# A second place for the first part's values, interleaved products of its last two units, and sixteen weight conversions moved into stage two

## The chip, the cores and the metric

The kernel runs on one core of a Trainium2 chip. The metric is the device time of one execution in microseconds (us). Of the kernel before, three executions are given, 863.11, 866.15 and 866.83 us, with a median of 866.15 us; one further execution was recorded by the profiler.

## The reference, cut to what matters

Three layers run one after the other: block-causal attention (4 batches, 8 heads, 576 tokens, 64 wide), a dense layer with a leaky ReLU, and a layer that sends each token to one of eight experts. The change concerns the second layer alone:

```
x = attn_out.transpose(0, 2, 1, 3).reshape(2304, 512)
h = x @ w_in                     # w_in 512 x 2048
g = maximum(0.01 * h, h)
y = g @ w_out                    # w_out 2048 x 512
```

The weights `w_in` and `w_out` come as 64-bit floats, and the kernel converts them on the chip.

## The kernel before, in words

**The split of the dense layer.** The 2048 columns of `w_in` (and rows of `w_out`) are cut into 512 columns that are done in stage one, beside and just after the attention (the "first part" of the layer, weights `wi_a`, `wo_a`), and 1536 that are done in stage two (`wi_b`, `wo_b`). Stage two's weights lie in six tiles `wbt0` to `wbt5` and fall again into a first, second and third part of 512 columns: `wbt0`/`wbt1` are its first part's `w_in`/`w_out`, `wbt2`/`wbt4` its second's, `wbt3`/`wbt5` its third's. `wbt0` and `wbt1` are also the attention's places for its queries and keys.

**A conversion** (`split64`, `split_words`, L391 to L420) loads 512 KB into one of three `raw` tiles (L398, SP's queue) and makes a high and a low fp32r tile of it. The steps are two on ScalarE (L413, L414), three on VectorE (L415, L416, L417), one on GpSimd (L418), then the high part on ScalarE (L419) and the low part on VectorE (L420). One part has eight conversions, four of `w_in` and four of `w_out`. While the list `gate` holds instructions, every instruction of a conversion stands behind the one of its engine in that list.

**A unit** of stage one is 384 tokens; there are six, 0 to 5 (`half_a_steps`). `mm1(f)`, four of them, each multiply 12 products into a PSUM bank `ph` (three products for each of four 128-row pieces: high x high, high x low, low x high), and `leaky` (L437 to L439) makes the values `gA` of it: ScalarE scales (L437, into a tile `cv2`), VectorE takes the maximum (L438), ScalarE rounds to the high part (L438 ACT), GpSimd subtracts for the low part (L439). `mm2(t)`, three of them, multiply `gA` with `wo_a`, 12 products each, into a bank `po`, which ScalarE copies out (L489) and SP's queue stores (L490). There is one pair of tiles `gA` for all units, so a unit's `leaky` waits for the unit before to have read it in all its `mm2`. Units 4 and 5 take their `ph` from the four banks with the tag `ps` that the attention uses too, and their small tiles from a pool `tr` with two buffers each.

**The order of the work.** Attention steps, units 0 to 3 and conversions carry due times and are sorted by them (`todo`). A scheduler that simulates a timeline then orders the instructions of each engine, so products of two groups can come interleaved. The attention's last pair ends with `pv` products (L285), the sum of its two halves (L298 on ScalarE, L299 on VectorE), a rounding (L301) and a low part (L302 on GpSimd); these write the last tokens of `xT`, which units 4 and 5 read. In the list the four `w_out` conversions of stage two's first part come at due times 33.0 to 33.6, between the attention's last steps, which end at 34.3. Then the attention's pools are closed, the pool `WB` (`wbt2` to `wbt5`) and the pool `tr` are opened, and units 4 and 5 follow one after the other, with five conversions of the second part between their steps (L535 to L540).

**Stage two** (L1036 to L1076) goes over 72 pairs of a unit of 384 tokens and a 128-column piece (the first 36 go to three units in turns, four pieces at a time): `b_mm1` (12 products and `leaky`) and, two steps later, `b_mm2` (9 products into `acc`). In two of three steps a conversion is taken from the list `wb` (L1043); when it is empty, `load_rows` (L598 to L604) loads the rows of the routing weights that the logits (L662) need from step 31 on. The pieces of the second part are first used in step 12, those of the third in step 24.

Of the kernel before, what the change touches and what calls it, by code (L numbers as in the profile page):

```python
# [11 lines left out]
F32R = mybir.dt.float32r  # L12
# [13 lines left out]
def run_all(steps):  # L26
    for s in steps:
        s()
# [318 lines left out]
def attention_moe_kernel(  # L347
# [21 lines left out]
    NFA, NFB = FA // 128, FB // 128  # L369
# [4 lines left out]
    BT = TB * 128  # L374
# [47 lines left out]
    def moe_weight_steps(f0, n, wi, wo, pin=False):  # L422

        steps = []
        for a in range(0, n, 4):
            for c in range(ND):
                steps.append(lambda a=a, c=c: split64(
                    wi[0][:, c, a * 128 : a * 128 + 512], wi[1][:, c, a * 128 : a * 128 + 512],
                    w_in[c * 128 : (c + 1) * 128, f0 + a * 128 : f0 + a * 128 + 512], pin))
            for f in range(a, a + 4):  # L430
                steps.append(lambda f=f: split64(
                    wo[0][:, f], wo[1][:, f], w_out[f0 + f * 128 : f0 + (f + 1) * 128], pin))
        return steps

    def leaky(pool, ph, N, gh, gl, bufs, name="u", width=0):
        u = pool.tile([128, max(N, width)], F32, name=name, bufs=bufs)[:, 0:N]
        nc.scalar.activation(out=u, in_=ph, func=AF.Copy, scale=0.01)  # L437
        return [nc.vector.tensor_tensor(out=u, in0=ph, in1=u, op=ALU.max), nc.scalar.copy(gh, u),  # L438
                nc.gpsimd.tensor_tensor(out=gl, in0=u, in1=gh.bitcast(F32), op=ALU.subtract)]  # L439

    def three(ps, a, b, first, last):

        n = len(a)
        m = 0
        for (ah, al), (bh, bl) in zip(a, b):
            for x, y in ((ah, bh), (ah, bl), (al, bh)):
                nc.tensor.matmul(ps, x, y, start=first and m == 0, stop=last and m == 3 * n - 1)  # L447
                m += 1
# [3 lines left out]
    right = ExitStack()  # L452
    ps1 = p1.enter_context(tc.tile_pool(name="ps1", bufs=1, space=PSUM))
    M1 = p1.enter_context(tc.tile_pool(name="m1", bufs=1))
    wi_a = [M1.tile([128, ND, FA], F32R, name=f"wia{i}") for i in range(2)]
    wo_a = [M1.tile([128, NFA, D], F32R, name=f"woa{i}") for i in range(2)]
    BAS = ((0, 256), (256, 320))
    gA = [M1.tile([128, NFA, BT], F32R, name=f"gA{i}") for i in range(2)]

    WA = ctx.enter_context(tc.tile_pool(name="wa", bufs=1, side="right"))  # L460
    wbt = [WA.tile([128, 2, 4 * 512], F32R, name=f"wbt{i}") for i in range(2)]
# [7 lines left out]

    where, a_ends = [CV, 512, 3], []  # L470

    def half_a_steps(u, tag="mm", bufs=2):

        o = u % 3 * BT

        def mm1(f):
            ph = ps1.tile([128, 512], F32, name="ph", tag=tag, bufs=bufs)[:, 0:BT]
            fs = slice(f * 128, f * 128 + 128)
            three(ph, [(wi_a[0][:, c, fs], wi_a[1][:, c, fs]) for c in range(ND)],
                  [(xT[0][:, c, o : o + BT], xT[1][:, c, o : o + BT]) for c in range(ND)], True, True)  # L480
            a_ends[:] = leaky(where[0], ph, BT, gA[0][:, f], gA[1][:, f], where[2], "cv2", where[1])

        def mm2(t):
            po = ps1.tile([128, 512], F32, name="po", tag="mm", bufs=2)
            ts = slice(t * 128, t * 128 + 128)
            three(po, [(gA[0][:, f, ts], gA[1][:, f, ts]) for f in range(NFA)],
                  [(wo_a[0][:, f], wo_a[1][:, f]) for f in range(NFA)], True, True)
            st = where[0].tile([128, 512], F32, name="cv3", bufs=where[2])
            a_ends[:] = [nc.scalar.copy(st, po)]  # L489
            nc.sync.dma_start(part_d[u * BT + t * 128 : u * BT + t * 128 + 128], st)  # L490

        return [lambda f=f: mm1(f) for f in range(NFA)] + [lambda t=t: mm2(t) for t in range(TB)]
# [8 lines left out]
    todo = att.steps(dst, LAG)  # L501
# [3 lines left out]
    for u, (t0, t1, n) in enumerate(((10.35, 17.15, 7), (17.15, 19.1, 4), (21.5, 26.2, 7), (26.35, 33.1, 7))):  # L505
        ha = half_a_steps(u)
        todo += [(t0 + (t1 - t0) * j / n, s) for j, s in enumerate(ha[:n])]
        todo += [(t1 + 0.7 * j, s) for j, s in enumerate(ha[n:])]
# [3 lines left out]
    end = per * B  # L512
# [4 lines left out]
    def wb_steps(a):  # L517

        wi, wo = ([wbt[at[a]][:, i].rearrange("p (c w) -> p c w", c=4) for i in range(2)] for at in (wi_at, wo_at))
        return moe_weight_steps(FA + a * 512, 4, wi, wo)  # L520

    wb = wb_steps(0)
    todo += [(end - 0.5 + 0.2 * j, s) for j, s in enumerate(wb[:4])]
    todo += [(end + 1 + 0.2 * j, s) for j, s in enumerate(wb[4:])]
    run_all(s for _, s in sorted(todo, key=lambda x: x[0]))
    right.close()
    gate[:] = a_ends
    right = ExitStack()
    WB = right.enter_context(tc.tile_pool(name="wb", bufs=1, side="right"))
    wbt += [WB.tile([128, 2, 4 * 512], F32R, name=f"wbt{i}") for i in range(2, 6)]  # L530
    behind = ExitStack()
    where[1:] = BT, 2
    where[0] = behind.enter_context(tc.tile_pool(name="tr", bufs=1, side="right"))
    wb = wb_steps(1) + wb_steps(2)
    for j, step in enumerate(half_a_steps(4, "ps", 4) + half_a_steps(5, "ps", 4)):  # L535
        step()
        if j in (4, 6, 8, 10, 12):

            gate[:] = a_ends
            wb.pop(0)()  # L540
    behind.close()
    p1.close()


# [289 lines left out]
    def load_expert(e):  # L834
# [4 lines left out]
        if k_ < 3:  # L839
            x, y = ((wo_at[0], wo_at[1]), (wi_at[2], wo_at[2]), (wi_at[0], wi_at[1]))[k_]  # L840
            a, b = ((WA if t < 2 else WB).tile([128, 2, 4 * 512], F32, name=f"wbt{t}").rearrange("p i w -> p (i w)") for t in (x, y))
            a, b = a.rearrange("p (c w) -> p c w", w=F2), b.rearrange("p (c k w) -> p c k w", k=2, w=D)
# [198 lines left out]
    for i in range(len(seq) + lag):  # L1041
# [11 lines left out]
        f = i - (len(seq) - NFB)  # L1053
# [16 lines left out]
        if i >= lag:  # L1070
            n, f = seq[i - lag]
# [29 lines left out]
    end = finish()  # L1101
# [110 lines left out]
```

## Time and profile before

| what | value |
|---|---|
| three executions | 863.11, 866.15, 866.83 us (median 866.15) |
| the profiled execution | 863.9 us, span 862.1 us from first to last instruction |
| PE busy in the span | 795.8 us (92%), 4100 products |
| mean granted TensorE clock | 0.980 |
| end of the attention's last product to stage two's first | 317.5 to 357.94 us |
| stage two up to its logits | 358 to 480 us, PE busy 121.57 of 122 us |

PE is TensorE's multiplying, PEld its weight load, DVE VectorE, ACT ScalarE, POOL GpSimd, SP the engine whose queue issues most DMAs. Times count from the start of the span. In a row of the timeline, "[2.36 <-ACT cv L489]" says that the engine was idle for 2.36 us before, and that an instruction of line 489 on ScalarE ended that. "x12" is the number of merged instructions. PEclk is the granted clock as a share of full speed.

### The profile page before, as it was taken

Reading aid. Unit: us, or ns where it says so; the run is one execution under the profiler, and the core shown is the slowest. Engines: PE = TensorE matmul, PEld = TensorE weight load, DVE = VectorE, ACT = ScalarE, POOL = GpSimd, SP = SyncE. Lnnn points to the kernel's source line nnn. Section 1 sums busy time; section 2 is a strip of 40 time slices with the busy share of each in tenths; the row PEclk is TensorE's granted clock in tenths of the full one; section 3 lists DMA queues with packets and bytes.
Section 4 is the critical chain, followed back from the end, with each engine's and each line's share of the span. In section 5 each row is a group of like instructions: output and inputs, shape, how many; then the busy total and the mean of one; then the engine's idle time right before and its main releaser. Section 6 shows DMA issues by size and latency. Waiting matters only on the chain. (4 is left out here: it accounts for less than half of the span.)

```text
span 862.1 us, 12392 instructions
## 1 busy us (share of the span) xinstructions
PE 795.8 (92%) x4100; PEld 651.2 (76%) x4100; DVE 518.6 (60%) x1131; ACT 397.6 (46%) x909; POOL 352.3 (41%) x427
## 2 busy tenths in 40 slices
PE   6788999999999989799999999999999969989995
PEld 4577787989889788588999988798998758544442
DVE  6886788888878794776522799977222722111111
ACT  5887788887878774654422212222233312101010
POOL 3765554463545664654323234354225331010210
PEclk9799999999999999999999999999999989999998
DMA  6664753474332152652400663123126651693910
GB/s 164 173 169 100 203 108 94 102 202 118 77 100 56 39 183 82 217 198 74 147 1 16 205 184 110 36 76 111 65 103 207 236 85 37 240 396 134 326 60 7
DMA packets 114653, 112.89 MB, mean 131 GB/s; under 512 B 76718, under 2 KB 79790, under 8 KB 114562
## 3 DMA queue, kind: packets, MB, share of 16 engines
q1 hardware_dynamic: 106386, 95.72, 36.7%
q0 software_dynamic: 8176, 16.06, 6.2%
q8 instruction: 44, 0.72, 0.3%
q14 instruction: 47, 0.39, 0.1%
HBM read 81.23 MB, written 22.70 MB: 121 GB/s over the span
## 5 line engine op out<-in xcount | busy, mean ns | idle before, releaser
L447 PE MATMUL ph<-xT,wbt 128*128 128x384 f32 x864 | 166.8, 338 | 5.0 <-DVE u L438 2.7
L447 PEld LDWEIGHTS ph<-xT,wbt 128*128 128x128 f32 x864 | 152.0, 188 | 14.8 <-DVE u L438 5.0
L439 POOL TENSOR_TENSOR gl<-u,gh 128x384 fp32r<-128x384 f32 x72 | 79.7, 1107 | 155.2 <-ACT gh L438 147.2
L447 PE MATMUL acc<-wbt,gh 128*128 128x512 f32 x432 | 132.9, 396 | 0.0
L185 POOL TENSOR_SCALAR P<-P,stat 128x128 f32<-128x128 f32 (+2 forms) x144 | 79.1, 572 | 76.1 <-DVE stat L183 52.8
L438 DVE TENSOR_TENSOR u<-ph,u 128x384 f32<-128x384 f32 x72 | 39.7, 551 | 89.7 <-ACT u L437 89.7
L438 ACT CAST gh<-u 128x384 fp32r<-128x384 f32 x72 | 36.9, 513 | 121.0 <-DVE u L438 52.7
L447 PEld LDWEIGHTS acc<-wbt,gh 128*128 128x128 f32 x432 | 79.8, 188 | 12.3
L447 PE MATMUL acc<-wbt,gl 128*128 128x512 f32 x216 | 81.9, 395 | 0.0
L285 PE MATMUL pv<-ph,vs 128*128 128x320 f32 (+4 forms) x280 | 70.7, 323 | 2.7 <-DVE ph L239 1.6
L236 PE MATMUL pt<-ident,P 128*128 128x128 f32 x400 | 62.7, 283 | 6.7 <-ACT P L174 2.5
L437 ACT ACTIVATE u<-ph 128x384 f32<-128x384 f32 x72 | 35.2, 489 | 70.6 <-PE ph L447 66.8
L161 PE MATMUL sp<-wbt 128*128 128x128 f32 (+2 forms) x192 | 57.1, 376 | 9.6 <-DVE ph L239 2.8
L447 PE MATMUL ph<-xT,wia 128*128 128x384 f32 x288 | 59.0, 351 | 2.8 <-DVE cv L438 2.0
L447 PE MATMUL po<-woa,gA 128*128 128x512 f32 x216 | 56.2, 403 | 3.5 <-ACT gA L438 2.8
L285 PEld LDWEIGHTS pv<-ph,vs 128*128 128x128 f32 x280 | 51.3, 193 | 9.1 <-DVE ph L239 2.7
L418 POOL TENSOR_TENSOR cv<-cv,cv 128x512 int32<-128x512 int32 x32 | 43.7, 1367 | 33.8 <-DVE cv L417 21.7
L236 PEld LDWEIGHTS pt<-ident,P 128*128 128x128 f32 x400 | 47.1, 144 | 12.8 <-ACT P L174 3.0
L662 DVE CUSTOM_DVE_ANT_0 xlast<-x,raw 128x512 f32<-128x512 f32 x72 | 55.0, 803 | 0.0
L447 PEld LDWEIGHTS ph<-xT,wia 128*128 128x128 f32 x288 | 51.5, 195 | 4.3 <-DVE cv L438 2.5
L243 DVE TENSOR_TENSOR pl<-pt,ph 128x512 fp32r<-128x512 f32 (+2 forms) x84 | 50.9, 624 | 5.1 <-ACT ph L242 4.1
L447 PEld LDWEIGHTS po<-woa,gA 128*128 128x128 f32 x216 | 39.9, 191 | 13.1 <-ACT gA L438 3.7
(244 smaller groups left out, 1533.9 us busy)
## 6 DMA issues: line engine op xcount, KB each, us to landing
wbt<-in_moe_w_dram SPq DMA_DIRECT2D x48, 512.0 KB, 7.7
wbt<-wbt SPq DMA_DIRECT2D x60, 144.0 KB, 2.6
raw<-in_moe_w_in_dram SPq DMA_DIRECT2D x16, 512.0 KB, 4.1
raw<-in_moe_w_out_dram SPq DMA_DIRECT2D x16, 512.0 KB, 4.1
xTd<-xT POOLq DMA_DIRECT2D x4, 1152.0 KB, 8.0
part_d<-cv SPq DMA_DIRECT2D x18, 256.0 KB, 2.1
x<-part_d SPq DMA_DIRECT2D x6, 768.0 KB, 7.9
xT<-xTd POOLq DMA_DIRECT2D x6, 768.0 KB, 7.4
```

Of the source, the lines that this page charges most:

```text
L161: nc.tensor.matmul(o_, st()[a][h][:, rows : rows + m], st()[b][:, h, c : c + w], start=(i == 0), stop=(i == 1))
L185: nc.gpsimd.tensor_scalar(out=P, in0=P, scalar1=rs[:, i : i + 1], scalar2=1.0, op0=ALU.mult, op1=ALU.mult)
L236: nc.tensor.transpose(o, src, self.ident)
L243: nc.vector.tensor_tensor(out=dl, in0=s_, in1=dh.bitcast(F32), op=ALU.subtract)
L285: nc.tensor.matmul(box["pv"][:, c0:N], v, box[t][:, i, h, cs], start=(jc == 0 and t == "ph"), stop=(jc == runs[-1][0] and t == parts[-1]))
L418: nc.gpsimd.tensor_tensor(out=w, in0=w, in1=low, op=ALU.add)
L437: nc.scalar.activation(out=u, in_=ph, func=AF.Copy, scale=0.01)
L438: return [nc.vector.tensor_tensor(out=u, in0=ph, in1=u, op=ALU.max), nc.scalar.copy(gh, u), nc.gpsimd.tensor_tensor(out=gl, in0=u, in1=gh. ...
L439: nc.gpsimd.tensor_tensor(out=gl, in0=u, in1=gh.bitcast(F32), op=ALU.subtract)]
L447: nc.tensor.matmul(ps, x, y, start=first and m == 0, stop=last and m == 3 * n - 1)
L662: nc.vector.tensor_tensor_reduce(out=junk, in0=x2[:, t], in1=wrow[j], scale=1.0, scalar=0.0, op0=ALU.mult, op1=ALU.add, accum_out=box["L"] ...
```

## The change

The tiles `gA` are made by a helper; unit 5 gets a pair of its own, in the pool `tr`. The four `w_out` conversions of stage two's first part leave the sorted list: they now come after the steps 3, 5, 8 and 10 of units 4 and 5, each behind the last `leaky` or copy so far. Units 4 and 5 are interleaved: four `mm1` of unit 4, two of unit 5, one `mm2` of unit 4, two `mm1` of unit 5, two `mm2` of unit 4, three `mm2` of unit 5. The pool `tr` is opened straight after the attention's pools are closed, and `WB` only after `tr` is closed. The five second-part conversions that ran in this stretch are gone from it: all sixteen conversions of the second and third part are in the list that stage two takes from. `load_rows`, behind the last of them, moves from stage two's step 15 to its step 22.

```diff
-    gA = [M1.tile([128, NFA, BT], F32R, name=f"gA{i}") for i in range(2)]
+    new_g = lambda pool: [pool.tile([128, NFA, BT], F32R, name=f"gA{i}") for i in range(2)]
+    gA = new_g(M1)
...
-    def half_a_steps(u, tag="mm", bufs=2):
+    def half_a_steps(u, tag="mm", bufs=2, gA=gA):
...
     wb = wb_steps(0)
     todo += [(end - 0.5 + 0.2 * j, s) for j, s in enumerate(wb[:4])]
-    todo += [(end + 1 + 0.2 * j, s) for j, s in enumerate(wb[4:])]
     run_all(s for _, s in sorted(todo, key=lambda x: x[0]))
     right.close()
     gate[:] = a_ends
+    behind = ExitStack()
+    where[1:] = BT, 2
+    where[0] = behind.enter_context(tc.tile_pool(name="tr", bufs=1, side="right"))
+    four, five = half_a_steps(4, "ps", 4), half_a_steps(5, "ps", 4, gA=new_g(where[0]))
+
+    both = four[:4] + five[:2] + four[4:5] + five[2:4] + four[5:] + five[4:]
+    wb = wb[4:]
+    for j, step in enumerate(both):
+        step()
+        if j in (3, 5, 8, 10):
+
+            gate[:] = a_ends
+            wb.pop(0)()
+    behind.close()
     right = ExitStack()
     WB = right.enter_context(tc.tile_pool(name="wb", bufs=1, side="right"))
     wbt += [WB.tile([128, 2, 4 * 512], F32R, name=f"wbt{i}") for i in range(2, 6)]
-    behind = ExitStack()
-    where[1:] = BT, 2
-    where[0] = behind.enter_context(tc.tile_pool(name="tr", bufs=1, side="right"))
-    wb = wb_steps(1) + wb_steps(2)
-    for j, step in enumerate(half_a_steps(4, "ps", 4) + half_a_steps(5, "ps", 4)):
-        step()
-        if j in (4, 6, 8, 10, 12):
-
-            gate[:] = a_ends
-            wb.pop(0)()
-    behind.close()
+    wb += wb_steps(1) + wb_steps(2)
     p1.close()
```

## Rows read from the trace of the kernel before

**Rows 1.** Page, first part: busy time of PE, share of the span, instructions.

```profile
PE 795.8 (92%) x4100; PEld 651.2 (76%) x4100; DVE 518.6 (60%) x1131; ACT 397.6 (46%) x909; POOL 352.3 (41%) x427
```

**Rows 2.** Busy time by stretch; first column start:end, then its length in us.

```profile
core 0: us, PE busy (x) PEld busy (x) DVE busy (x) ACT busy (x) POOL busy (x), PEclk, DMA share, GB/s
290.00:296.00 6.00, 3.86 (x26) 2.78 (x25) 5.94 (x13) 4.53 (x12) 2.71 (x3) 1.00 0.34 93
...
318.21:329.72 11.51, 9.47 (x34) 8.51 (x34) 10.35 (x15) 6.88 (x14) 7.43 (x7) 0.70 0.34 113
329.72:357.94 28.22, 22.45 (x101) 17.58 (x100) 16.00 (x28) 15.36 (x30) 13.92 (x19) 1.00 0.34 120
358.00:480.00 122.00, 121.57 (x614) 109.90 (x615) 57.66 (x99) 48.57 (x94) 47.89 (x50) 1.00 0.34 107
```

**Rows 3.** Timeline of PE, 315 to 374 us: start, us, work, [idle before].

```profile
315.95 0.42 PE L285 MATMUL pv<-ph,vs 128*128 128x320 f32 x1 [0.92 <-DVE tm L299]
...
317.19 0.28 PE L285 MATMUL pv<-pl,vs 128*128 128x64 f32 x1
318.21 3.90 PE L447 MATMUL ph<-xT,wia 128*128 128x384 f32 x12 [0.74 <-DVE xT L301]
324.15 2.20 PE L447 MATMUL ph<-xT,wia 128*128 128x384 f32 x9 [2.04 <-DVE cv L438]
...
339.74 5.64 PE L447 MATMUL po<-woa,gA 128*128 128x512 f32 x24
345.98 2.07 PE L447 MATMUL po<-woa,gA 128*128 128x512 f32 x6 [0.59 <-ACT gA L438]
350.28 1.83 PE L447 MATMUL po<-woa,gA 128*128 128x512 f32 x6 [2.23 <-ACT gA L438]
352.56 3.02 PE L447 MATMUL po<-woa,gA 128*128 128x512 f32 x12 [0.44 <-ACT cv L489]
357.94 4.43 PE L447 MATMUL ph<-xT,wbt 128*128 128x384 f32 x24 [2.36 <-ACT cv L489]
```

**Rows 4.** Groups of products on PE from 318.2 to 357.9 us.

```profile
L447 PE MATMUL po<-woa,gA 128*128 128x512 f32 x72 | 19.6, 413 | 3.4 <-ACT gA L438 2.8 <-ACT cv L489 0.4
L447 PE MATMUL ph<-xT,wia 128*128 128x384 f32 x60 | 14.2, 388 | 2.8 <-DVE cv L438 2.0 <-DVE xT L301 0.7
```

**Rows 5.** Timeline of ACT, 320 to 358 us.

```profile
320.26 0.85 ACT L298 COPY tm<-pv 64x320 f32<-64x320 f32 x2
321.14 0.87 ACT L437 ACTIVATE cv<-ph 128x384 f32<-128x384 f32 x2
...
349.72 0.51 ACT L438 CAST gA<-cv 128x384 fp32r<-128x384 f32 x1 [2.89 <-DVE cv L438]
...
356.78 0.62 ACT L419 CAST wbt<-cv 128x512 fp32r<-128x512 f32 x1 [1.65 <-POOL cv L418]
357.31 0.58 ACT L489 COPY cv<-po 128x512 f32<-128x512 f32 x1
```

**Rows 6.** Timeline of DVE, 306 to 481 us.

```profile
306.66 0.32 DVE L301 CAST xT<-tm 128x320 fp32r<-128x320 f32 x1
...
315.48 0.42 DVE L299 TENSOR_TENSOR tm<-pv,tm 64x256 f32<-64x256 f32 x1
...
316.79 1.36 DVE L301 CAST xT<-tm 128x256 fp32r<-128x256 f32 x1
...
480.91 0.68 DVE L662 CUSTOM_DVE_ANT_0 xlast<-x,raw 128x512 f32<-128x512 f32 x1
```

**Rows 7.** Groups on POOL and DVE from 315 to 358 us: conversion (L418) and leaky.

```profile
L418 POOL TENSOR_TENSOR cv<-cv,cv 128x512 int32<-128x512 int32 x8 | 12.3, 1549 | 5.8 <-ACT cv L414 3.4 <-DVE cv L417 2.4
L439 POOL TENSOR_TENSOR gA<-cv,gA 128x384 fp32r<-128x384 f32 x8 | 9.0, 1128 | 14.9 <-ACT gA L438 14.9
L438 DVE TENSOR_TENSOR cv<-ph,cv 128x384 f32<-128x384 f32 x8 | 4.3, 553 | 5.4 <-ACT cv L437 5.4
```

**Rows 8.** SP's queue, the last load of the routing rows.

```profile
426.84 0.32 SPq L603 DMA_DIRECT2D cv<-wr_d  x1
```

## The prediction, made before the changed kernel was run

> **What bounds the kernel now.** The first part of the page comes first: PE multiplies for 92% of the span [rows 1], so a change can gain only what PE idles or loses in clock, and must be placed. The table by stretch says where: from 358 to 480 us PE is busy for 121.57 of 122 us, while from 318.21 to 357.94 us it is busy for 31.92 of 39.73 us, and in the first 11.51 us of that the mean granted clock is 0.70 [rows 2]. That stretch is exactly what the change rewrites. PE's timeline there is read next for the idle time before each piece. From 315.03 us (0.92 us before the piece at 315.95) to stage two's first product at 357.94 there are seven gaps: 0.92, 0.74, 2.04, 0.59, 2.23, 0.44 and 2.36 us, together 9.32 us [rows 3]. The released-by notes name VectorE or ScalarE each time, never a DMA. The last reading is why those two are late. ScalarE adds up the attention's last halves only at 320.26 us although their products ended at 317.47, and its first two leaky steps of unit 4 follow at 321.14; its last copy of `po` stands behind a conversion's L419, which had waited 1.65 us for GpSimd [rows 3, 5]. So PE waits for queues in which a conversion, itself waiting for another engine, stands in front.
>
> **The least this stretch can take.** After 317.47 us PE has 60 products of `ph` and 72 of `po` to do [rows 4]. At full clock 24 of the first took 4.43 us and 24 of the second 5.64 us [rows 3], so 0.185 and 0.235 us each: 60 x 0.185 + 72 x 0.235 = 28.0 us. With the 1.52 us of `pv` products before them that is 29.5 us of the 42.9 us from 315.03 to 357.94. The excess is 13.4 us: 9.3 us of gaps and some 4.1 us in which products ran at half clock (1.2 instead of 2.4 GHz). This is the bound of the gain here; there is none to be had in stage two, where 0.43 us are idle.
>
> **The change, part by part.**
>
> *Four conversions leave the attention's last steps.* Until 318 us VectorE's sum at 315.48 and the rounding at 316.79 [rows 6] stand behind their steps, and PE waits 0.92 and 0.74 us for just these two. The 2.04 us before 324.15 wait for unit 4's first maximum, behind ScalarE's late L437. With only attention work ahead, `pv` can go on at once and unit 4's first leaky follows its last products directly: scale 0.435 us, maximum 0.553 us [rows 5, 7]. The twelve products before it belong to four banks, so PE still has nine of them, 9 x 0.185 = 1.7 us, while the first bank is emptied; the attention's own sums and rounding share the two engines. I keep 0.7 us of these 3.70 us (bounds 0 and 3.70, nearer the lower as 1.0 us of work stands against 1.7 us of cover).
>
> *The half clock.* It came after two gaps that took 1.66 of 3.18 us, and again after the 2.04 us one [rows 3]. Between 290 and 296 us PE was also idle for 2.14 of 6.00 us, in smaller pieces, and the granted clock stayed at 1.00 [rows 2]. With the gaps down to 0.7 us I keep 0 of the 4.1 us; the bounds are 0 and 4.1.
>
> *Unit 5's own `gA`.* Now its leaky waits until unit 4's three `mm2` have read: 24 of their products run from 339.74 to 345.38 us, and then 0.59, 2.23 and 0.44 us follow in which PE waits for roundings and copies [rows 3]. The 2.23 us are VectorE's: the rounding at 349.72 waited 2.89 us for its maximum [rows 5]. With a second pair the values of unit 5 can be made while unit 4's 36 products run, 36 x 0.235 = 8.5 us; on GpSimd, the slowest of the chain, four low parts take 4 x 1.13 = 4.5 us and two conversions' L418 3.1 us [rows 7], so 7.6 us of work under 8.5 us of cover. That is tight: I keep 1.0 of 3.26 us, and another 1.0 us for a wait at the start of unit 4's `mm2`, whose values run through the same chain with only two buffers.
>
> *The hand-over to stage two.* After the last `po` product one copy of 0.58 us must run [rows 5]; the last conversion is now placed three `mm2` (36 products, 8.5 us) ahead, so it is through by then. Of 2.36 us I keep 0.65.
>
> *The interleaving itself.* It is worth nothing alone: unit 5's 48 products already run before 339.74, that is before most of unit 4's `mm2`.
>
> *The pool `tr` moves* into the space that the attention's tiles have just left. Unit 4's small tiles then wait for whatever lay there. By the tile sizes that is mostly the transposed probabilities of the last pair, read last by the `pv` products that end at 317.47. Leaky starts later than that in any case, so 0; were it the sum tile, read until the attention's last low part, up to 2 us.
>
> *Five conversions go to stage two*, with their five loads of 512 KB on SP's queue. VectorE is busy for 57.66 of 122 us there, ScalarE for 48.57, GpSimd for 47.89, with eleven conversions [rows 2]. Even if all of VectorE's time were theirs, five more would add 57.66 x 5/11 = 26.2 us, which makes 83.9 of 122. A step of stage two is 21 products and takes 12 x 0.185 + 9 x 0.235 = 4.3 us; the next use of a bank `ph` is two steps off, against 1.0 us for scale and maximum. Sixteen conversions at two in three steps end in step 22: the second part's last `w_in` one in step 4 (used in step 12), its last `w_out` one in step 10 (used in step 17), the third part's likewise 8 and 7 steps ahead, some 30 us. I take 0; the bounds are 0 and, if each of the five held a maximum back by one L418, 5 x 1.55 = 7.7 us. The loads of the routing rows move back seven steps, 30 us, as do those queued behind them; the last was issued at 426.84 and the first logit began at 480.91 [rows 6, 8], so of 54 us some 24 stay.
>
> **The sum.** 13.4 us less 0.7, 1.0, 1.0 and 0.65 is a gain of 10.0 us. The profiled execution took 863.9 us, 2.25 us under the median of 866.15; it would become 853.9, and the median 856.1 us, which is the forecast. Nothing later gives it back in the views read: stage two has no idle time that waits for a fixed hour, and the loads after it hang on its own steps.
>
> **Rivals.**
>
> *Only the second `gA` pays (0.20).* The scheduler fills the attention's end with other work, so that 3.70 us of gaps and the half clock stay. For it: four `w_in` conversions still fall due there, and VectorE is busy for 10.35 of 11.51 us [rows 2]. Against it: the steps in front of the sum and the rounding were largely the conversions that leave. The gain would be 3.26 + 1.7 = 5.0 us, so 861.2 us.
>
> *The clock drops all the same (0.10).* Small waits at the banks, between two units' groups of products, keep the half clock for a stretch like that of 318 to 330 us. The gain would be 10.0 - 4.1 = 5.9 us, so 860.3 us. The rows for 290 to 296 us speak against it, those from 318 us for it. The Trainium skill, in "TensorE: Matmul & The Clock Gate", section "A second HAM failure mode: psum-queue depth-cycling", speaks for this rival: cycling through PSUM banks, it says, made TensorE pause briefly between groups so often that its clock went back and forth. By that rule the sum would be 860.3 instead of 856.1 us; the trace has both cases, so it stays the smaller chance.
>
> *It moves nothing (0.05).* The simulated order puts unit 4's `mm2` on PE ahead of values that come late on the chip, and PE waits as long in another place: within 4 us of 866 us.
>
> *Slower: stage two waits for its routing rows (0.05).* VectorE works in order, so a logit that waits for its row holds the maxima behind it, and PE with them. It decides once the loads move by more than 54 us instead of 30, that is if conversions come at one in three steps rather than two. Twelve more steps would make it 30 + 52 = 82 us, 28 us too late; less the 10.0 us gain that is 18 us more, 884 us. Against it stands that eleven conversions now cost stage two 0.43 us.
>
> **How the numbers follow.** The forecast, a gain between 7 and 13.4 us, has 0.60. The range takes in its bound at the low end, 863.9 - 13.4 = 850.5, rounded to 851, and reaches up over the first two rivals and their spread to 863.5; nothing moved, slower, and the tails are left out. About 0.5%, or 4.3 us, is what a measurement can tell from no change. Faster by more than that: 0.60, most of 0.20 and of 0.10, so 0.80. Within it: the rest of these, the case that nothing moves, 0.14. Slower: 0.06 with what I overlook.
>
> **What would show it.** In the changed profile the first product of stage two should come near 348 us; `pv` should end before 317 us with no gap over 0.5 us ahead of it; the granted clock should stay at 1.00 from 318 to 330; no rounding of unit 5 should wait for a `po` product; the last copy of `po` should follow its product within 0.7 us. Stage two should keep under 1 us of idle time before its logits. The forecast is wrong if the gaps return under other names, if the clock row still shows 0.70, or if stage two's step grows past 4.3 us.

## The result, and where the time came from

The changed kernel takes 853.77 us (median of 5 executions, 852.12 to 858.10) against 866.15 us; the ratio is 0.9855 with a 95% interval of 0.9821 to 0.9888. The forecast was 856.1 us, in a range of 851.0 to 863.5. The profiled execution took 852.55 us, its span is 850.8 us.

Busy time by stretch in the changed kernel (columns as in [rows 2]): the attention's last products, the two units after it, stage two up to its logits.

```profile
314.90:317.82 2.92, 2.92 (x23) 2.92 (x23) 1.30 (x4) 0.42 (x1) 0.73 (x1) 1.00 0.00 1
317.82:347.55 29.73, 27.73 (x135) 23.87 (x133) 17.86 (x33) 18.11 (x36) 17.23 (x25) 1.00 0.41 144
...
347.60:469.60 122.00, 121.17 (x613) 109.61 (x614) 65.67 (x112) 56.63 (x108) 53.13 (x51) 1.00 0.37 117
```

Where [rows 2] had 39.73 us from unit 4's last 12 products of `ph` to stage two, 7.81 us of them without a product, there are 29.73 us with 2.00 without one, and the granted clock is 1.00 in all three rows. Stage two took the five conversions (VectorE 65.67 instead of 57.66 us of 122) and idles for 0.83 us instead of 0.43.

PE's timeline in the changed kernel, the pieces that answer to [rows 3]:

```profile
317.71 0.28 PE L285 MATMUL pv<-pl,vs 128*128 128x64 f32 x1
317.82 2.34 PE L447 MATMUL ph<-xT,wia 128*128 128x384 f32 x12
321.44 4.45 PE L447 MATMUL ph<-xT,wia 128*128 128x384 f32 x24 [1.28 <-DVE cv L438]
...
333.90 12.94 PE L447 MATMUL po<-woa,gA 128*128 128x512 f32 x55
347.55 4.43 PE L447 MATMUL ph<-xT,wbt 128*128 128x384 f32 x24 [0.72 <-ACT cv L490]
352.81 0.60 PE L596 MATMUL py<-ident,wg 128*9 128x128 f32 x4 [0.82 <-DMA wg<-in_moe_w_gate_dram]
```

The gaps of 0.92 and 0.74 us are gone; twelve products that took 3.90 us take 2.34; 55 products of `po` run without a pause where three gaps were. What stays is 1.28 us before unit 5, 0.72 us at the hand-over and a new 0.82 us in stage two, for the small load of the routing weights.

ScalarE and VectorE in the changed kernel, for [rows 5, 6]:

```profile
318.02 0.42 ACT L298 COPY tm<-pv 64x320 f32<-64x320 f32 x1 [0.85 <-PE pv L285]
320.31 0.87 ACT L437 ACTIVATE cv<-ph 128x384 f32<-128x384 f32 x2 [1.86 <-POOL xT L302]
...
346.92 0.59 ACT L490 COPY cv<-po 128x512 f32<-128x512 f32 x1 [0.81 <-PE po L447]
```

```profile
315.04 0.42 DVE L299 TENSOR_TENSOR tm<-pv,tm 64x256 f32<-64x256 f32 x1
315.49 0.29 DVE L301 CAST xT<-tm 128x256 fp32r<-128x256 f32 x1
```

The attention's last halves are now summed as soon as they are there, and the last copy waits only for its product. But the first leaky waits 1.86 us for the attention's last low part.

For the comparisons below one stretch is used: from the piece of 16 products that opens unit 4 (it stands at 306.32 us before, at 307.95 us after) to stage two's first product. It holds the same products in every kernel, and leaves out the attention up to its last `pv` products, whose length differs between executions. Before, then changed:

```profile
306.32:357.94 51.62, 42.16 (x200) 36.10 (x198) 38.09 (x62) 31.14 (x60) 27.84 (x30) 0.93 0.37 126
```

```profile
307.95:347.55 39.60, 37.60 (x199) 33.74 (x197) 24.52 (x47) 23.09 (x47) 20.84 (x29) 1.00 0.38 132
```

The stretch is 12.02 us shorter, where the medians differ by 12.4 us. The two profiled executions differ by 11.35 us (863.9 and 852.55): in the changed kernel the stretch starts 1.63 us later, 1.50 of it for a half clock in the attention that the last section shows. PE's idle time falls from 51.62 - 42.16 = 9.46 to 2.00 us, which is 7.46 us; its busy time for the same products falls by 4.56 us. Of these the clock (0.93 to 1.00) is the larger part: [rows 2] have 0.70 over 11.51 us, which is a loss of at most 11.51 x 0.30 = 3.45 us. The rest lies in pieces that ran longer at a granted clock of 1.00, such as the two pieces of six `po` products behind the gaps of 0.59 and 2.23 us, 2.07 and 1.83 us [rows 3], where six took 1.55 us in the same execution:

```profile
330.25 1.55 PE L447 MATMUL po<-woa,gA 128*128 128x512 f32 x6
```

### The profile page after: what moved, and what is told of

Same layout as the page of the kernel before. It is cut to its first block, busy times and chain, and to the rows that moved or that the text cites. A ratio compares the mean times of both kernels' runs of the same rounds, so it can differ in the third digit from the quotient of the medians.

```text
span 850.8 us, 12392 instructions
## 1 busy us (share of the span) xinstructions
PE 792.6 (93%) x4100; PEld 650.0 (76%) x4100; DVE 514.8 (61%) x1131; ACT 397.2 (47%) x909; POOL 350.3 (41%) x427
## 5 line engine op out<-in xcount | busy, mean ns | idle before, releaser
L285 PE MATMUL pv<-ph,vs 128*128 128x320 f32 (+4 forms) x280 | 68.9, 316 | 1.8 <-DVE ph L239 1.6
L437 ACT ACTIVATE u<-ph 128x384 f32<-128x384 f32 x72 | 35.1, 488 | 65.0 <-PE ph L447 59.3
L418 POOL TENSOR_TENSOR cv<-cv,cv 128x512 int32<-128x512 int32 x32 | 42.2, 1323 | 42.3 <-DVE cv L417 34.2
L447 PE MATMUL ph<-xT,wia 128*128 128x384 f32 x288 | 56.4, 341 | 1.3 <-DVE cv L438 1.3
L447 PEld LDWEIGHTS ph<-xT,wia 128*128 128x128 f32 x288 | 49.4, 188 | 2.1 <-DVE cv L438 1.6
L1006 PE MATMUL ph<-wbt,cv 128*128 128x512 f32 x96 | 43.6, 597 | 4.4 <-PEq L1154 3.0
```

The costliest lines, as they stand in the source:

```text
L285: nc.tensor.matmul(box["pv"][:, c0:N], v, box[t][:, i, h, cs], start=(jc == 0 and t == "ph"), stop=(jc == runs[-1][0] and t == parts[-1]))
L418: nc.gpsimd.tensor_tensor(out=w, in0=w, in1=low, op=ALU.add)
L1006: tc.keep_in_program_order(nc.tensor.matmul(ph[f], lx["xw"][:, c], a[c][:, f * 512 : f * 512 + 512], start=(c == 0), stop=(c == ND - 1)))
```

## The experiments

The table gives all runs. "Four" are the first-part conversions: at the attention's end, as before, or among the units' steps, as changed. In all rows but the first and f_four_back the sixteen others are in stage two. "Tile" is the unused tile of the fourth run. In the kernel before and in the rows marked * unit 5 follows unit 4; in the others the two are interleaved. Stretch and PE's busy time come from one profile each, the ratio to the kernel before from the timed executions. Up to stage two e_pad and g_rows_late are the same kernel, and their stretches agree within 0.01 us.

| kernel | four | gA | tile | stretch, us | PE busy | clock | ratio, 95% interval |
|---|---|---|---|---|---|---|---|
| before (five among the units) | end | 1 | - | 51.62 | 42.16 | 0.93 | 1 |
| a_five_only * | end | 1 | no | 50.89 | 40.19 | 0.93 | 1.0004 (0.998 to 1.0028) |
| b_conv_back | end | 2 | no | 50.50 | 40.17 | 0.93 | 0.9989 (0.9964 to 1.0015) |
| c_one_ga * | units | 1 | no | 44.88 | 38.72 | 1.00 | 0.994 (0.9911 to 0.9969) |
| changed | units | 2 | no | 39.60 | 37.60 | 1.00 | 0.9855 (0.9821 to 0.9888) |
| a_pad * | end | 1 | yes | 46.47 | 40.92 | 0.93 | 0.9943 (0.9914 to 0.9971) |
| b_pad | end | 2 | yes | 45.97 | 41.01 | 0.93 | 0.9941 (0.991 to 0.9972) |
| c_pad * | units | 1 | yes | 43.75 | 38.73 | 1.00 | 0.9896 (0.9864 to 0.9928) |
| e_pad | units | 2 | yes | 38.53 | 37.62 | 1.00 | 0.9855 (0.9815 to 0.9894) |
| d_pad * | units | 2 | yes | 38.72 | 37.81 | 1.00 | 0.9871 (0.9824 to 0.9919) |
| f_four_back (eight among the units) | units | 2 | no | 46.30 | 38.16 | 0.98 | 0.9939 (0.9913 to 0.9966) |
| g_rows_late | units | 2 | yes | 38.52 | 37.61 | 1.00 | 0.9915 (0.9878 to 0.9952) |

**Only the five conversions moved (a_five_only).** The pool `tr` stays where the change put it.

```diff
+    todo += [(end + 1 + 0.2 * j, s) for j, s in enumerate(wb[4:])]
...
-    four, five = half_a_steps(4, "ps", 4), half_a_steps(5, "ps", 4, gA=new_g(where[0]))
+    four, five = half_a_steps(4, "ps", 4), half_a_steps(5, "ps", 4)
...
-    both = four[:4] + five[:2] + four[4:5] + five[2:4] + four[5:] + five[4:]
+    both = four + five
-    wb = wb[4:]
+    wb = []
...
-        if j in (3, 5, 8, 10):
+        if j < 0:
```

> Only the five second-part conversions go to stage two; the four of the first part stay between the attention's last steps, the two units share one gA and follow one another. My theory (the conversions at the attention's end cost 3.7 us of gaps and the half clock 4.1 us; the shared gA 3.3 us; the hand-over 1.7 us): the gaps of 0.92, 0.74 and 2.04 us and the 0.70 clock stay, the hand-over gap shrinks from 2.36 to about 0.7 us and one of the gaps of 0.59 and 2.23 us may shrink too: a gain of 2 to 4 us over the kernel before. Rival (the five conversions in the units' stretch are the main cost): a gain of 8 us or more.

Neither came: there is no gain (864.66 us, ratio 1.0004). The gaps of 0.59 and 2.23 us are gone and the hand-over is 0.72 us, but another gap has grown. PE's and ScalarE's timelines of this kernel:

```profile
322.86 2.61 PE L447 MATMUL ph<-xT,wia 128*128 128x384 f32 x12 [1.26 <-DVE xT L301]
332.87 5.86 PE L447 MATMUL ph<-xT,wia 128*128 128x384 f32 x21 [7.40 <-DVE cv L438]
```

```profile
324.89 0.86 ACT L298 COPY tm<-pv 64x320 f32<-64x320 f32 x2
...
330.61 0.62 ACT L419 CAST wbt<-cv 128x512 fp32r<-128x512 f32 x1 [3.35 <-POOL cv L418]
331.73 0.49 ACT L437 ACTIVATE cv<-ph 128x384 f32<-128x384 f32 x1 [0.50 <-POOL xT L302]
```

Unit 4's first leaky (L437) again ends its wait with L302, the attention's last low part, which in turn stands behind the conversions. In the kernel before, with `tr` further down, two leaky steps ran right after L298 [rows 5]. This pointed to the place of the pool `tr`.

**The four conversions put back (b_conv_back)**, with the first and the last two changes of the diff above alone.

> The changed kernel, with the four first-part conversions put back between the attention's last steps. My theory: the gaps before 324 us and the low clock come back, so 6 to 8 us slower than the changed kernel, about 5 us faster than the kernel before. Rival (only the second gA and the interleaving pay): within 2 us of the changed kernel.

864.53 us, with the same gap of 7.41 us: the conversions' place does decide, the second `gA` does not pay alone, but the size is larger than my terms, since the pool's place adds to it.

**One gA (c_one_ga)**, with the second and third change of that diff alone: one pair of `gA`, and unit 5 after unit 4.

> The changed kernel with one gA for both units and the units one after the other; the nine conversions stay where the change put them. My theory: the attention's end and the clock are mended as in the changed kernel, the waits of unit 5's roundings for unit 4's products come back: 3 to 4 us slower than the changed kernel, about 8 us faster than the kernel before. Rival (only the second gA pays): 8 us or more slower than the changed kernel.

860.04 us, a stretch 5.28 us longer than the changed kernel's: my theory's direction, a larger size.

**The pool moved off (e_pad).**

```diff
+    behind.enter_context(tc.tile_pool(name="pad", bufs=1, side="right")).tile([128, 9216], F32, name="pad")
     where[0] = behind.enter_context(tc.tile_pool(name="tr", bufs=1, side="right"))
```

> The changed kernel with an unused 36 KB tile ahead of the pool tr, so that its tiles lie over attention tiles that were read last some 10 us earlier. If unit 4's first leaky (20.3 us past 300, behind the attention's last low part) is late because its pool lies over the attention's last tiles, the gap of 1.28 us before unit 5's first product goes and the time falls by about 1.3 us. If it is late because the engines are busy or for the scheduler's order, the gap and the time stay as they are.

In this kernel the leaky waits for its product, and the gap on PE is 0.19 us:

```profile
323.62 0.87 ACT L437 ACTIVATE cv<-ph 128x384 f32<-128x384 f32 x2 [0.77 <-PE ph L447]
```

```profile
324.76 4.45 PE L447 MATMUL ph<-xT,wia 128*128 128x384 f32 x24 [0.19 <-DVE cv L438]
```

The stretch is 1.07 us shorter. The median (853.79 us) does not show it; an interval of 0.4% is some 3.4 us either way. So it is a version no worse than the changed one, and shown better only in the stretch.

**The other three kernels with the tile (a_pad, b_pad, c_pad)**, and **the interleaving undone (d_pad)** by `both = four + five` with two `gA`.

> As the run with only the five conversions moved (four conversions back at the attention's end, one gA, one unit after the other), with the unused 36 KB tile ahead of the pool tr. Measured from the 16-product piece of unit 4's first products to stage two's first product: 51.62 us before, 50.89 without the unused tile. If the 7.40 us gap there came of the pool lying over the attention's last tiles, it falls to about 2 us and the stretch to 45 to 47 us. If it came of the conversions' order alone, the stretch stays at 50 us or more.

> The changed kernel with the four conversions back at the attention's end and the unused tile: only the second gA, the interleaving and the five moved conversions, with the pool out of the attention's way. Same stretch: 50.50 us without the unused tile, 39.60 in the changed kernel. If the four conversions still cost what I said (3.7 us of gaps and some half clock), 43 to 46 us. If they cost nothing once the pool is away, 39 to 40 us.

> The changed kernel with one gA, one unit after the other, and the unused tile. Same stretch: 44.88 us without the unused tile. If the pool's place and the second gA are separate costs, 43.8 us (1.1 less, as in the run with the tile alone); if the wait for the attention's tiles is hidden here, 44.9.

> The changed kernel with the unused tile and both gA, but the steps of unit 5 listed after all steps of unit 4. Same stretch: 38.53 us with the interleaving. My step in the prediction says that the interleaving is worth nothing alone: 38 to 39.5 us. Rival (the interleaving is what fills the chain of values): 2 us or more longer.

All four lie where the theory put them. a_pad has 46.47 us: the 7.40 us gap fell to 2.19, so 4.4 us were the pool lying where the attention's last steps, themselves held up by conversions, still read. b_pad has 45.97 us, so the four conversions' place is worth 45.97 - 38.53 = 7.44 us with two `gA`. Its PE timeline shows how:

```profile
320.92 3.86 PE L447 MATMUL ph<-xT,wia 128*128 128x384 f32 x12 [1.25 <-DVE xT L301]
326.85 2.60 PE L447 MATMUL ph<-xT,wia 128*128 128x384 f32 x9 [2.08 <-DVE cv L438]
...
354.50 4.43 PE L447 MATMUL ph<-xT,wbt 128*128 128x384 f32 x24 [0.72 <-ACT cv L490]
```

The gaps of before are back, and so is the half clock: 12 products in 3.86 us, against 2.34. The second `gA` and the interleaving are worth 46.47 - 45.97 = 0.50 us here. In c_pad, where the four conversions stand among the units' steps, they are worth 43.75 - 38.53 = 5.22 us, the second `gA` without the interleaving 43.75 - 38.72 = 5.03 (d_pad, below). What one `gA` costs there is on PE:

```profile
341.11 1.21 PE L447 MATMUL po<-woa,gA 128*128 128x512 f32 x4 [0.98 <-ACT gA L438]
342.48 2.33 PE L447 MATMUL po<-woa,gA 128*128 128x512 f32 x8 [0.16 <-POOL gA L439]
345.25 3.01 PE L447 MATMUL po<-woa,gA 128*128 128x512 f32 x12 [0.44 <-ACT cv L490]
351.51 5.78 PE L447 MATMUL ph<-xT,wbt 128*128 128x384 f32 x24 [3.25 <-ACT cv L490]
```

The 3.25 us are a copy of `po` that is late; in the same kernel without the tile its wait of 3.33 us is for a store buffer. ScalarE in c_one_ga:

```profile
354.29 0.58 ACT L490 COPY cv<-po 128x512 f32<-128x512 f32 x1 [3.33 <-DMA part_d<-cv]
```

SP's queue in c_one_ga shows why the store was late:

```profile
343.42 5.84 SPq L398 DMA_DIRECT2D raw<-in_moe_w_in_dram  x3
349.36 0.86 SPq L491 DMA_DIRECT2D part_d<-cv  x2
```

Three loads of conversions occupy the queue for 5.84 us (the longest wait among them is 4.6 us, for the L417 of a conversion), and two stores of `po` stand behind them. So by these rows the hand-over's 3.25 - 0.72 = 2.53 of the 5.2 us come of conversions once more, through a store, and only the smaller pauses (0.98, 0.16 and 0.44 us) show the values of unit 5 coming late.

In d_pad the stretch is 0.19 us longer than in e_pad: with two `gA`, interleaving the steps adds next to nothing.

**Four more conversions among the units' steps (f_four_back).**

```diff
+    right = ExitStack()
+    WB2 = right.enter_context(tc.tile_pool(name="wb2", bufs=1, side="right"))
+    wbt.append(WB2.tile([128, 2, 4 * 512], F32R, name="wbt2"))
...
-    wb = wb[4:]
+    hi, lo = (wbt[2][:, i].rearrange("p (c w) -> p c w", c=4) for i in range(2))
+    wb = wb[4:] + [lambda c=c: split64(hi[:, c], lo[:, c], w_in[c * 128 : (c + 1) * 128, FA + 512 : FA + 1024]) for c in range(ND)]
...
-        if j in (3, 5, 8, 10):
+        if j in (3, 4, 5, 6, 8, 9, 10, 11):
...
-    wb += wb_steps(1) + wb_steps(2)
+    wb += wb_steps(1)[4:] + wb_steps(2)
...
```

> The changed kernel with the second part's four w_in conversions back in the units' stretch (eight conversions there instead of four, their target in a pool of its own, which also keeps the pool tr off the attention's last read tile). Same stretch from the 16-product piece to stage two: 39.60 us in the changed kernel, 38.53 with the unused tile. Theory (the units' stretch has ScalarE, VectorE and GpSimd busy for some 18 of 30 us; four more conversions take 8 us of ScalarE, 9 to 12 of VectorE with its waits, 6 of GpSimd and so leave no room): gaps before unit 5's second products or the hand-over come back, 41 to 44 us. Rival (with two gA there is room for them): 38.5 to 40 us.

862.95 us, and a stretch of 46.30 us: there is no room for them, and the price is higher than expected. PE and ScalarE in this kernel:

```profile
344.22 6.13 PE L447 MATMUL po<-woa,gA 128*128 128x512 f32 x25 [2.20 <-POOL gA L439]
354.67 8.74 PE L447 MATMUL ph<-xT,wbt 128*128 128x384 f32 x36 [4.33 <-ACT cv L490]
```

```profile
353.51 0.62 ACT L419 CAST wbt<-cv 128x512 fp32r<-128x512 f32 x1 [1.65 <-POOL cv L418]
354.04 0.58 ACT L490 COPY cv<-po 128x512 f32<-128x512 f32 x1
```

The last copy stands behind an L419 that waits for GpSimd, just as at the hand-over of the kernel before [rows 5]. The expectation was wrong on one point: the gap of 1.28 us stayed (1.29). In ScalarE's timeline the first leaky again waits for L302:

```profile
320.74 0.87 ACT L437 ACTIVATE cv<-ph 128x384 f32<-128x384 f32 x2 [1.86 <-POOL xT L302]
```

Yet `tr` lies here, by the tile sizes, over the attention's value tile, its statistics and the probabilities `ph0` and `ph1`, and not over the sum tile that L302 reads. So the wait seems to go with the attention's pool `at` as a whole, and not with the one tile; in e_pad `tr` lies wholly over the attention's other pool, and does not wait. This is worked out from the tile sizes in kernel.py; no run tried it by itself.

**Routing rows made late (g_rows_late).** The kernel is e_pad, with the loads held until the first unit's result is stored:

```diff
...
-                load_rows()
...
+        if i == 30:
+            with tc.issue_after(kept[0].ins):
+                load_rows()
```

> The changed kernel with the unused tile, and the loads of the routing rows held back on SP's queue until the first unit's result of stage two is stored (issued at about 475 us where the first logit now begins at 471, instead of 430 to 444). This makes late what my slower rival says is late. By that rival VectorE stops at the first logits for the loads' landing (some 8 to 12 us), holds the maxima behind it, and PE loses several us there: 4 to 10 us slower than without. If VectorE's backlog is made up before its next use counts, the time stays within 2 us.

858.53 us, 4.7 us over e_pad, with intervals that overlap a little; so the waits decide. VectorE's first logit in this kernel, and PE's longest waits after it (to 700 us), then those of e_pad:

```profile
478.47 0.69 DVE L667 CUSTOM_DVE_ANT_0 xlast<-x,raw 128x512 f32<-128x512 f32 x1 [2.92 <-DMA raw<-wr_d]
```

```profile
PE ph L447 <- DVE u L438: 4.6, 5, 1.4
PE py L920 <- DVE hl L968: 4.3, 1, 4.3
PE acc L447 <- POOL gl L439: 2.2, 2, 1.3
```

```profile
PE py L920 <- DVE hl L968: 2.9, 1, 2.9
PE ph L447 <- DVE u L438: 2.2, 4, 0.7
```

Counted from stage two's first product the logits begin 478.47 - 345.91 = 132.6 us in, against 473.6 - 350.87 = 122.7 in e_pad: 9.8 us late cost about half of that by the medians, and by the waits listed 11.1 - 5.1 = 6.0 us. The price is there; in the changed kernel no logit waits for a load.

## Why the prediction was right, step by step

**The place and the bound held.** The excess of 13.4 us was put at 9.3 us of gaps and 4.1 us of half clock; 7.46 us of idle and 4.56 of busy time came back. The forecast kept 3.35 us of gaps; 2.00 stayed. The split by cause is another matter. With the pool out of the way the stretch falls by 5.15 us for the five conversions (51.62 to a_pad's 46.47), by 0.50 for the second `gA` and the interleaving (b_pad) and by 7.44 for the four conversions (e_pad); the pool's place takes 1.07 back, which leaves the 12.02. Another order of the steps would split it otherwise, as c_pad shows. One sign that the prediction named failed: the last `pv` product ended at 317.99 us and not before 317, since everything came 1.63 us later, mostly for the half clock in the attention.

**Four conversions at the attention's end: right and the largest part.** 3.70 us of gaps and the clock were named for them; with the pool out of the way and two `gA` their place is worth 7.44 us (b_pad to e_pad), 4.05 of idle and 3.39 of busy time, where the terms make 3.0 + 4.1 = 7.1.

**The half clock: right in this stretch, mis-sized, and on evidence that does not carry it.** The 4.1 us were what was left over when the gaps were taken off; [rows 2] give 3.45. That the clock would stay was argued from 290 to 296 us, where it stood at 1.00 with 2.14 us idle. In the changed kernel the same pieces, with the same gaps, were followed by a half clock (last section). What the profiles do show is the stretch itself: its granted clock is 0.93 in all five kernels with the four conversions at the attention's end, and 1.00 in all six that have only these four among the units.

**Unit 5's own `gA`: the gaps went, but for another reason.** The step said that "its leaky waits until unit 4's three `mm2` have read", and gave it 2.26 us. In a_five_only and a_pad, with one `gA`, the gaps of 0.59 and 2.23 us do not occur. So what made them was the five conversions in VectorE's and ScalarE's queues, which the step on those conversions priced only in stage two, at 0, and not by what their leaving gives: 5.15 us, with the hand-over. The second pair does something else: it lets the four conversions stand among the units' steps. Without it their move gives 46.47 - 43.75 = 2.72 us, with it 7.44.

**The hand-over: right.** 0.65 us were kept, 0.72 measured; f_four_back brings the old hand-over back by putting conversions last again.

**The pool `tr`: mis-sized.** The step took 0 "By the tile sizes", with 2 us as the bound if it were the sum tile. It costs 1.07 us in the changed kernel. As far as f_four_back tells, the first writer in `tr` waits for the last reader of the whole pool it was laid over, whichever of its tiles lie beneath. Where the conversions hold the attention's end up, the same place costs 4.4 us.

**The two waits of 1.0 us inside the units** did not occur; the 0.7 us before unit 5's first bank is 0.19 us when the pool is away.

**The interleaving is worth nothing alone: right** (0.19 us). **The five conversions in stage two: right**, 0.83 us of idle time, 0.82 of it for the routing weights' load, which the prediction did not see.

**The rivals.** "Only the second `gA` pays" fell with b_conv_back (0.9989) and b_pad. "The clock drops all the same" fell for this stretch: the clock row is 1.00 with gaps of 1.28 and 0.72 us. The Trainium skill's section "A second HAM failure mode: psum-queue depth-cycling" ("TensorE: Matmul & The Clock Gate"), which spoke for it, does not describe this stretch: PE went on through the same banks, in two units' turns, at full clock. "Slower" had its mechanism right and its margin as forecast: 24 us were to be left, and the loads and logits of the changed kernel stand 27.2 us apart, by SP's queue and by VectorE's logits (duration in ns, then first and last start):

```profile
443.57 0.32 SPq L607 DMA_DIRECT2D cv<-wr_d  x1
```

```profile
L666 DVE CUSTOM_DVE_ANT_0 xlast<-x,raw x72: 656/681/1885, 470.8 to 579.8; 128x512 f32<-128x512 f32 x72
```

## What to carry to other kernels

A conversion that crosses three engines costs little where the bounding engine has a long queue of ready work and the others have room, and much at a seam between two stages, where each engine's next short step is what the other waits for; move it out of the seam before speeding up the seam's own steps. Edits at a seam do not add: the second buffer was worth 0.5 us alone and 5.2 us beside the moved conversions, so try them together before one is dropped. A tile pool opened on space just freed can inherit the last reader of the whole old pool; look at what the first writer in it waits for.

## What the runs showed of the hardware

VectorE's rounding of 128x256 took 0.29 us in the changed kernel, at 315.49, with GpSimd idle until 315.86; in the kernel before it took 1.36 us [rows 6], ending at 318.15 beside this GpSimd step, which ended at 318.00 (GpSimd's timeline before):

```profile
316.54 1.46 POOL L418 TENSOR_TENSOR cv<-cv,cv 128x512 int32<-128x512 int32 x1
```

The Trainium skill, "SBUF — State Buffer", section "SBUF: two separate sides", says that the two engines share a port pair as an exclusive lock: a GpSimd step and a VectorE step in a two-port mode (or with two SBUF inputs, against a GpSimd step that reads SBUF) keep each other out for a whole instruction. These rows agree: the rounding ended 0.15 us after the step beside it. Which mode it ran in no run shows. So a conversion at the seam held VectorE twice, by its own steps and through GpSimd's.

Of the clock the runs show no line in the size of a gap. The half clock followed two gaps of 0.92 and 0.74 us (12 products in 3.90 us), while 24 products after one of 2.36 us took 4.43 us, as at full clock [rows 3]; after one of 3.25 us (c_pad) they took 5.78. The same gaps can even go either way. PE's pieces near 296 us, in the kernel before and then in the changed one:

```profile
294.99 0.30 PE L236 MATMUL pt<-ident,P 128*128 128x128 f32 x1 [0.85 <-DVE pl L243]
295.92 0.51 PE L236 MATMUL pt<-ident,P 128*128 128x128 f32 x2 [0.63 <-ACT P L177]
296.43 3.02 PE L447 MATMUL po<-woa,gA 128*128 128x512 f32 x12
```

```profile
295.13 0.30 PE L236 MATMUL pt<-ident,P 128*128 128x128 f32 x1 [0.85 <-DVE pl L243]
296.06 0.54 PE L236 MATMUL pt<-ident,P 128*128 128x128 f32 x2 [0.63 <-ACT P L177]
296.57 4.52 PE L447 MATMUL po<-woa,gA 128*128 128x512 f32 x12
```

All twelve profiles have these gaps, and in seven of them the twelve `po` products behind took 4.27 to 4.61 us, in five 3.02 to 3.04. So 1.5 us of what two executions of this program differ by can be the clock in a place that no edit touched; a change of that size is to be read from the stretch that it concerns. Why the clock fell in one and not in the other stays open.
